# A one-token gated block: ScalarE takes small steps from VectorE, wider value weights, b1 added after the product, a wo tail of twelve rows

## The chip, the cores and the metric

The kernel runs on one core of a Trainium2 chip. The metric is the device time of one execution in microseconds; the median of three runs is 131.92 us (131.88 to 132.19). One core has five engines that run side by side, each with its own program: TensorE (PE; its weight loads are shown apart as PEld), VectorE (DVE), ScalarE (ACT), GpSimd (POOL) and SyncE (SP), which here only issues DMAs. Sixteen DMA engines move data between memory and the core's buffers. Engines wait for each other and for transfers through semaphores.

## What is computed

One token `x` of 576 values goes through two branches that a gate mixes. Branch A is attention over the last 4,096 positions of a key and value cache (32 query heads on 16 key heads, 128 values each). Branch B is a dense layer with GELU, 576 to 4,608 and back. All inputs are bfloat16.

```python
g = sigmoid((x * gate_w).sum(-1))
q = (x @ wq).reshape(heads=32, 128)
k, v = k_cache[:, -4096:], v_cache[:, -4096:]      # 16 heads, each for two query heads
p = softmax(q @ k.T * 128 ** -0.5)
a = (p @ v).reshape(4096) @ wo
h = gelu(x @ w1 + b1)
b = h @ w2 + b2
out = g * a + (1 - g) * b
```

Nearly every byte is read once: 53.6 MB of weights and cache.

## The kernel before

**Stages.** The weights come first: w1 and then wq, each spread over 128 partitions. TensorE multiplies them with `x2`, the token laid out by partition (L404, helper `spread`, four products side by side in column groups of the array). The h row is turned into columns by VectorE (L434), goes through GELU on VectorE and ScalarE (L436 to L460) and ends as `gt`, 36 columns. The q row is turned in the same way and put into `qz_flat`.

**Keys and values.** The 16 key heads are taken in four tiles of four heads (`g` from 0 to 3). For each tile SyncE loads keys (`k_t`) and later values (`v_t`), 4 MB each. VectorE transposes keys in two halves into `kt` (L542), TensorE makes the scores (L564) on top of a product that sets foreign heads to a very low number (L551). `row_max` takes each row's maximum on VectorE (L580), spreads it into 16 columns (`mr`, L583), and TensorE brings it to all rows of a head (L589); `exps` takes the minimum (L597), and ScalarE the exponentials (L601); `probs` transposes them into `pt` (L613). `values(g)` multiplies 32 chunks of weights from `pt`, 32 columns each, with the values (L656), into one bank of 512 columns. `pick(g)` keeps from these only what belongs to each row's own head, with four VectorE operations (L677, L684) and the mask `own4`. `fold(g)` adds up the rows on TensorE (L697) into `o_ps`.

**The end.** The attention result, divided by the sums and times the gate, is made into columns for wo. Of the 128 rows of wo for each head, the first 4 x RW (RW = 30) come as `wo_t`, 30 rows for a partition, and the last RT = 8 rows of each head as `wo_tail`, one partition for each head, in three transfers of 11, 11 and 10 heads (L645). `om` and `om_t` (L766, L771) hold the matching columns; products at L779 and L784 move them into `ov_ps`, and VectorE and ScalarE copy them out as `ov` and `ov_tail`. Then `y_add` (L386) adds vector times matrix row by row into `y_ps`, two products for each of these vectors, one for either half of the 576 outputs. The list `late` sets their order: the vectors of w2's first half that are left (14 to 17), those of `wo_tail`, one product whose result nothing reads (L807), those of `wo_t`, those of w2's second half. ScalarE and VectorE each copy one half of the row out, and SyncE stores it.

**Order.** TensorE and VectorE work off programs whose order is partly set by hand: `queue` chains the emission of each engine's operations in the attention part. Pools with a fixed number of buffers decide when a tile may be loaded: `kt_pool` has two buffers, shared in turn by `rows`, `turn`, the `kt` halves and `wo_tail`; the big tiles go by tags, so that `v_t` of tile 0 takes the place of `k_t` of tile 0, w2 that of `k_t` of tile 2 (before it w1), `v_t` of tile 3 that of `v_t` of tile 0, and `wo_t` that of `v_t` of tile 1. SyncE issues all large transfers in one order: w1, wq, four `k_t`, two `v_t`, half of w2, `v_t` of tile 2, the three of `wo_tail`, `v_t` of tile 3, `wo_t`, and three pieces of w2's second half (vectors 0 to 9, 10 to 15, 16 and 17). ScalarE issues the short rows x, gate_w, b2 and b1.

**b1.** It comes as two rows of 2,304. Eight small products (L404, weights from `ident`) put it into `h_ps` before the products of w1 add to it.

Of the kernel before, what the change touches and what calls it, by code (L numbers as in the profile page):

```python
# [9 lines left out]
FP32 = mybir.dt.float32  # L10
BF16 = mybir.dt.bfloat16
# [7 lines left out]
def kernel(  # L19
# [15 lines left out]
    nc = tc.nc  # L35
# [169 lines left out]

    rows = kt_pool.tile([2, 8192], BF16, name="rows", tag="kt")
    x_row = rows[0:1, 0:D]
    gw_row = rows[0:1, D : 2 * D]
    b2_row = rows[0:1, 2 * D : 3 * D]
    b1_t = rows[0:2, 3 * D : 3 * D + FH]  # L210
    xdup = rows[0:1, 3 * D + FH : 5 * D + FH]
    junk_row = rows[0:1, 5 * D + FH : 6 * D + FH]
    nc.scalar.dma_start(out=x_row, in_=A_x.rearrange("a b d -> (a b) d"))
    nc.scalar.dma_start(out=gw_row, in_=gate_w.rearrange("(o n) -> o n", o=1))
    nc.scalar.dma_start(out=b2_row, in_=B_b2.rearrange("(o n) -> o n", o=1))
    nc.scalar.dma_start(out=b1_t, in_=B_b1.rearrange("(h n) -> h n", h=2))

# [8 lines left out]

    NCC = 2 * NI + 16 + P + 4
    low = const.tile([P, NCC], I32, name="low")
    mask = const.tile([P, NCC], I32, name="mask")
    c0 = 0  # L230
    for base, pattern, keep in (
        (0, [[1, NI], [1, 2]], 1),
        (128, [[-8, 16]], 120),
        (128, [[-1, P]], 7),
        (128, [[-8, 4]], 24),
    ):
        n = 1
        for step, num in pattern:
            n *= num
        nc.gpsimd.iota(low[:, c0 : c0 + n], pattern=pattern, base=base, channel_multiplier=1)  # L240
        nc.gpsimd.memset(mask[:, c0 : c0 + n], keep)
        c0 += n
# [9 lines left out]
    make_identity(nc, ident[:])  # L252
    RW = 30
    RT = P - 4 * RW
    NZ = 512 + 5 * RW + P
    ROWS = NZ + 32 * NI
# [48 lines left out]
    same8 = is0[:, c0 + 16 : c0 + 16 + P]  # L305
    own4 = is0[:, c0 + 16 + P : NCC]
    row_of = zeros[0:HB, ROWS : ROWS + 32 * HB].rearrange("p (r b m) -> p r b m", r=16, b=HB)
# [21 lines left out]

    nc.vector.tensor_copy(  # L330
        out=xdup.rearrange("p (d t) -> p d t", t=2),
# [3 lines left out]
    for i in range(NI):  # L335
# [27 lines left out]
    nc.scalar.activation(out=ge[:], in_=g_ps[:, 0:1], func=ACT.Exp, scale=-1.0)  # L363
    nc.vector.tensor_scalar(out=ge[:], in0=ge[:], scalar1=1.0, scalar2=None, op0=ALU.add)
    g_t = const.tile([P, 1], FP32, name="g_t")
# [5 lines left out]
    b2g = const.tile([1, D], FP32, name="b2g")  # L371
    nc.vector.tensor_scalar(
        out=b2g[:], in0=b2_row, scalar1=omg[0:1, 0:1], scalar2=None, op0=ALU.mult
    )
    gh = const.tile([P, 1, 5], FP32, name="gh")
    nc.vector.tensor_scalar(
        out=gh[:, 0, :], in0=hi5[:], scalar1=g_t[:, 0:1], scalar2=None, op0=ALU.mult
    )

# [23 lines left out]
    def spread(out, lhsT, rhs, start, stop):  # L403
        nc.tensor.matmul(out, lhsT=lhsT, rhs=rhs, start=start, stop=stop, skip_group_check=True)  # L404

    for u in range(2):
        for c in range(4):
            n0 = c * FG + u * FS
            spread(
                h_ps[32 * c : 32 * c + 32, u, 0:FS],  # L410
                ident[0:2, 0:32],
                b1_t[:, n0 : n0 + FS],
                True,
                False,
            )
    QZ = 24
    qz_flat = const.tile([P, QZ + 4 * NG * P + 96], BF16, name="qz_flat")
    nc.gpsimd.memset(qz_flat[:].bitcast(FP32), 0.0)
    for i in range(NI):
        for u in range(2):  # L420
            for c in range(4):
                n0 = c * FG + u * FS
                spread(
                    h_ps[32 * c : 32 * c + 32, u, 0:FS],
                    x2[:, i, :],
                    w1_t[:, i, n0 : n0 + FS],
                    False,
                    i == NI - 1,
                )
    turn = kt_pool.tile([P, 8192], BF16, name="turn", tag="kt")  # L430
    flat = turn[:].bitcast(FP32)
    h_row, h_col, q_col = flat[:, 0:FG], flat[:, FG : FG + 32 * NJ], flat[:, 2048 : 2048 + 512]
    nc.scalar.copy(out=h_row.rearrange("p (u n) -> p u n", u=2), in_=h_ps[:, :, 0:FS])  # L433
    nc.vector.transpose(out=h_col, in_=h_row.rearrange("p (m j) -> p j m", j=NJ))  # L434
    hacc = const.tile([P, NF], FP32, name="hacc")
    nc.vector.tensor_copy(  # L436
        out=hacc[:].rearrange("p (t j) -> p t j", t=2),
        in_=h_col.rearrange("p (j a) -> p a j", a=32)[:, 0:2, :],
    )
    z2 = const.tile([P, NF], FP32, name="z2")  # L440
    nc.vector.tensor_tensor(out=z2[:], in0=hacc[:], in1=hacc[:], op=ALU.mult)
    C0 = 0.7978845608028654
# [12 lines left out]
    nc.scalar.activation(out=e_h[:], in_=u_t[:], func=ACT.Exp, scale=-1.0)  # L455
    nc.vector.tensor_scalar(out=e_h[:], in0=e_h[:], scalar1=1.0, scalar2=None, op0=ALU.add)
    r_t = const.tile([P, NF], FP32, name="r_t")
# [49 lines left out]

    m1 = const.tile([P, 1], FP32, name="m1")
    mr = const.tile([P, 16], FP32, name="mr")
    negm = const.tile([P, 1], FP32, name="negm")  # L510
    sums = const.tile([P, NG, 1], FP32, name="sums")
# [67 lines left out]
    def row_max(g):  # L579
        queue("dve", lambda: nc.vector.reduce_max(out=m1[:], in_=s_ps[g][:], axis=AX.X))  # L580
        queue(
            "dve",
            lambda: nc.vector.tensor_scalar(  # L583
                out=mr[:], in0=hi16[:], scalar1=m1[:, 0:1], scalar2=None, op0=ALU.mult
            ),
        )
        queue(
            "pe",
            lambda: nc.tensor.matmul(  # L589
                mt_ps[:, 16 * g : 16 * g + 16], lhsT=same8, rhs=mr[:], start=True, stop=True  # L590
            ),
        )

    def exps(g):
        queue(
            "dve",
            lambda: nc.vector.tensor_reduce(  # L597
                out=negm[:], in_=mt_ps[:, 16 * g : 16 * g + 16], axis=AX.X, op=ALU.min
            ),
        )  # L600
        nc.scalar.activation(  # L601
            out=p_t[:].rearrange("p c k -> p (c k)"),
            in_=s_ps[g][:],
            func=ACT.Exp,
            bias=negm[:, 0:1],
            scale=SCALE,
            accum_out=sums[:, g, :],
        )
# [34 lines left out]
    for r in range(3):  # L643
        n = min(11, Hq - 11 * r)
        nc.sync.dma_start(  # L645
            out=wo_tail[32 + r : 32 + r + 4 * n - 3 : 4, 0 : RT * D],
            in_=wo_src[11 * r : 11 * r + n, 4 * RW : P, :].rearrange("h j n -> h (j n)"),
        )
    o_ps = ps_m.tile([P, Hq, 1], FP32, name="o_ps", tag="m")

    v_ps, v_own = [None] * NG, {}

    def value_products(g):
        for c in range(32):
            m = c % 4
            last = nc.tensor.matmul(  # L656
                v_ps[g][32 * m : 32 * m + 32, 0:512],
                lhsT=pt[:, g, c, :],
                rhs=v_t[g][:].rearrange("p (x c) d -> p x c d", x=4)[:, :, c, :],
                start=(c < 4),  # L660
                stop=(c >= 28),
                skip_group_check=True,
            )
        return last
# [4 lines left out]

    own_pool = ctx.enter_context(tc.tile_pool(name="own_pool", bufs=2))  # L670

    def pick(g):
        v_own[g] = own_pool.tile([P, Dh], FP32, name="v_own", tag="own")
        parts = v_ps[g][:, 0:512].rearrange("p (x d) -> p x d", x=4)
        queue(
            "dve",
            lambda: nc.vector.tensor_scalar(  # L677
                out=v_own[g][:], in0=parts[:, 0, :], scalar1=own4[:, 0:1], scalar2=None, op0=ALU.mult
            ),
        )  # L680
        for x in range(1, 4):
            queue(
                "dve",
                lambda x=x: nc.vector.scalar_tensor_tensor(  # L684
                    out=v_own[g][:],
                    in0=parts[:, x, :],
                    scalar=own4[:, x : x + 1],
                    in1=v_own[g][:],
                    op0=ALU.mult,
                    op1=ALU.add,  # L690
                ),
            )

    def fold(g):
        queue(
            "pe",
            lambda: nc.tensor.matmul(  # L697
                o_ps[:, 8 * g : 8 * g + 8, 0],
                lhsT=v_own[g][:],
                rhs=same8[:, 0:8],  # L700
                start=True,
                stop=True,
                skip_group_check=True,
            ),
        )
# [5 lines left out]
    probs(NG - 1)  # L711
    pick(0)
    ls = const.tile([P, NG, 8], FP32, name="ls")
# [4 lines left out]
        op=ALU.mult,  # L718
    )
    values(1)  # L720
    fold(0)
# [46 lines left out]
    )  # L768
    for r in range(3):
        n = min(11, Hq - 11 * r)  # L770
        nc.vector.tensor_tensor(  # L771
            out=om_t[:, 32 + r : 32 + r + 4 * n - 3 : 4],
            in0=o_ps[:, 11 * r : 11 * r + n, 0],
            in1=rgh[:, 11 * r : 11 * r + n, 4],
            op=ALU.mult,
        )
    ov_ps = ps_m.tile([P, RO + RT], FP32, name="ov_ps", tag="m")
# [74 lines left out]
```

## Time and profile before

| | |
|---|---|
| median of three runs | 131.92 us (131.88 to 132.19) |
| the profiled execution | 132.06 us, span of its instructions 130.8 us |
| TensorE busy | 72.3 us (55%), 572 products; weight loads 26.2 us, 462 |
| VectorE busy | 59.1 us (45%), 68 instructions |
| ScalarE busy | 9.0 us (7%), 19 instructions |
| GpSimd busy | 10.3 us (8%), 27 instructions |
| read from memory | 53.62 MB, 410 GB/s over the span |
| DMA queue of SyncE | 2,226 packets, 96.1% of the sixteen engines' span |

The span runs from the first to the last instruction of the profiled execution. Busy shares are means over stages with different limits. A line such as `L656` is a line of the kernel before. The clock column gives the share of full speed that TensorE was granted; it is 1.0 or 0.5 here. A landing is the moment at which a transfer's semaphore has its full count; each DMA engine that takes part adds its own count when its packets are written.

### The profile page before, as it was taken

What the parts mean: (1) busy time and instruction counts of PE and PEld (TensorE: products, weight loads), DVE (VectorE), ACT (ScalarE), POOL (GpSimd) and SP (SyncE); (2) the same over time, 40 slices, a digit from 0 to 9 for tenths busy, and PEclk for the clock granted to TensorE, in tenths of its full rate; (3) what the DMA queues carried; (4) which work ended last, traced back from release to release, by engine and by line L of the source; (5) the groups of instructions that cost most, each with busy time, mean ns of one, the idle gap of its engine ahead of it and who ended that gap; (6) DMA issues with size and microseconds to landing.
All of it is one profiled execution on the core that took longest, in us unless ns stands there. A gap on an engine that the chain in (4) does not pass through costs nothing.

```text
span 130.8 us, 1234 instructions
## 1 busy us (share of the span) xinstructions
PE 72.3 (55%) x572; PEld 26.2 (20%) x462; DVE 59.1 (45%) x68; ACT 9.0 (7%) x19; POOL 10.3 (8%) x27
## 2 busy tenths in 40 slices
PE   0002259460003997769949927985100980678794
PEld 0002103130000221211211211132000360234572
DVE  0023300360079979999999995046500050042001
ACT  2100000113000000030011003003000000000001
POOL 5005940000000000000000060000000000000000
PEclk9999999996555799986999995599955586579999
DMA  7999899899999999999989999999999999999970
GB/s 216 495 471 432 375 428 474 361 461 456 401 421 481 411 401 471 421 391 471 441 381 461 461 401 421 423 415 453 461 401 411 471 431 397 476 391 388 416 284 5
DMA packets 2241, 53.70 MB, mean 411 GB/s; under 512 B 278, under 2 KB 282, under 8 KB 540
## 3 DMA queue, kind: packets, MB, share of 16 engines
q1 hardware_dynamic: 2226, 53.61, 96.1%
q8 instruction: 4, 0.07, 0.2%
q10 hardware_dynamic: 10, 0.01, 0.0%
q14 instruction: 1, 0.01, 0.0%
HBM read 53.62 MB, written 0.00 MB: 410 GB/s over the span
## 4 chain that ended last, share of the span: by engine, by line
DMA 61%; DVE 21%; PE 9%; issue 5%; SPq 2%; ACT 1%; DVEq 0%; ACTq 0%
DMA k_t<-in_A_k_cache_dram 34%; DMA w_t<-in_B_w_dram 27%; DVE kt L542 15%; PE s_ps L564 5%; PE v_ps L656 3%; DVE m L580 3%; DVE pt L613 2%; ACT p_t L601 1%; PE y_ps L386 1%; DVE mr L583 1%; SPq L530 0%; SPq L758 0%; SPq L763 0%; ACT out_row L819 0%; DVE negm L597 0%
## 5 line engine op out<-in xcount | busy, mean ns | idle before, releaser
L564 PE MATMUL s_ps<-kt,qz_flat 128*128 128x512 bf16 x128 | 34.9, 433 | 19.4 <-DVE kt L542 12.6
L542 DVE STREAM_TRANSPOSE kt<-k_t 128x4096 f32<-128x4096 f32 x8 | 35.3, 4432 | 8.8 <-DMA k_t<-in_A_k_cache_dram 8.8
L656 PE MATMUL v_ps<-v_t,pt 128*32 128x512 bf16 x128 | 11.0, 505 | 14.8 <-DMA v_t<-in_A_v_cache_dram 13.3
L564 PEld LDWEIGHTS <-qz_flat 128*128 128x128 bf16 x64 | 7.1, 111 | 44.4 <-issue 42.9
L677 DVE TENSOR_SCALAR v_own<-v_ps,is 128x128 f32<-128x128 f32 x4 | 1.4, 338 | 20.0 <-PE v_ps L656 20.0
L601 ACT ACTIVATE p_t<-s_ps,negm 128x1024 bf16<-128x1024 f32 x4 | 4.5, 1114 | 53.8 <-DVE negm L597 53.8
L656 PEld LDWEIGHTS <-pt 128*32 128x32 bf16 x128 | 3.9, 117 | 20.2 <-DMA v_t<-in_A_v_cache_dram 13.4
L336 PE MATMUL xs_ps<-ident,rows 1*128 1x1 bf16 x9 | 0.6, 189 | 12.2 <-POOL ident masks.py:199 12.2
L642 POOL MEMSET wo_tail<- 128x2304 f32 x1 | 2.0, 2017 | 58.2 <-PE s_ps L564 58.2
L580 DVE TENSOR_REDUCE m<-s_ps 128x1 f32<-128x1024 f32 x4 | 4.8, 1196 | 4.0 <-PE s_ps L564 4.0
L386 PE MATMUL y_ps<-w_t,gt 128*1 128x272 bf16 (+1 forms) x72 | 6.0, 288 | 0.2 <-DMA w_t<-in_B_w_dram 0.2
L613 DVE STREAM_TRANSPOSE pt<-p_t 128x1024 bf16<-128x1024 bf16 x4 | 4.9, 1225 | 2.7 <-ACT p_t L601 2.7
L434 DVE STREAM_TRANSPOSE turn<-turn 128x576 f32<-128x576 f32 x1 | 1.3, 1255 | 9.5 <-ACT turn L433 9.5
L820 DVE CAST out_row<-y_ps 1x272 bf16<-1x272 f32 x1 | 0.4, 429 | 10.1 <-PE y_ps L386 10.1
L386 PE MATMUL y_ps<-wo_t,ov 128*1 128x272 bf16 (+1 forms) x60 | 4.0, 286 | 0.8 <-DMA wo_t<-in_A_wo_dram 0.8
L684 DVE SCALAR_TENSOR_TENSOR v_own<-v_ps,is,v_own 128x128 f32<-128x128 f32 x12 | 4.1, 342 | 0.3
L404 PE MATMUL h_ps<-w_t,zeros 128*32 128x288 bf16 x72 | 4.1, 420 | 0.0
L551 PE MATMUL s_ps<-foreign,zeros 4*128 4x512 bf16 x8 | 3.0, 433 | 2.1 <-POOL foreign L319 2.1
L386 PEld LDWEIGHTS <-gt 128*1 128x1 bf16 x72 | 3.7, 85 | 2.1 <-issue 1.1
L404 PEld LDWEIGHTS <-zeros 128*32 128x32 bf16 (+1 forms) x76 | 2.5, 119 | 7.3 <-issue 4.2
L330 DVE COPY rows<-rows 1x1152 bf16<-1x1152 bf16 x1 | 0.7, 748 | 6.9 <-DMA rows<-in_A_x_dram 6.9
L386 PEld LDWEIGHTS <-ov 128*1 128x1 bf16 x60 | 3.4, 84 | 2.0 <-issue 1.6
(78 smaller groups left out, 40.6 us busy)
## 6 DMA issues: line engine op xcount, KB each, us to landing
k_t<-in_A_k_cache_dram SPq DMA_DIRECT2D x4, 4096.0 KB, 37.7
v_t<-in_A_v_cache_dram SPq DMA_DIRECT2D x4, 4096.0 KB, 23.3
w_t<-in_B_w_dram SPq DMA_DIRECT2D x1, 5184.0 KB, 15.0
wq_t<-in_A_wq_dram SPq DMA_DIRECT2D x1, 4608.0 KB, 25.1
wo_t<-in_A_wo_dram SPq DMA_DIRECT2D x1, 4320.0 KB
w_t<-in_B_w_dram SPq DMA_DIRECT2D x1, 2592.0 KB
w_t<-in_B_w_dram SPq DMA_DIRECT2D x1, 1440.0 KB
w_t<-in_B_w_dram SPq DMA_DIRECT2D x1, 864.0 KB
```

The lines of the kernel that those rows point to most:

```text
L386: last = nc.tensor.matmul(y_out[s], lhsT=vec, rhs=row[:, DH:D] if s else row[:, 0:DH], start=start, stop=stop, skip_group_check=True,)
L404: nc.tensor.matmul(out, lhsT=lhsT, rhs=rhs, start=start, stop=stop, skip_group_check=True)
L542: lambda: nc.vector.transpose(out=kt[g, f][:].bitcast(FP32), in_=keys.rearrange("p c d -> p (c d)").bitcast(FP32),),
L551: nc.tensor.matmul(s_ps[g][:, u * 512 : (u + 1) * 512], lhsT=row_of.rearrange("p r b m -> p (r b m)"), rhs=foreign[:].rearrange("p n b -> ...
L564: last = nc.tensor.matmul(s_ps[g][:, u * 512 : (u + 1) * 512].rearrange("p (c k) -> p c k", k=32), lhsT=qz(g, j, 2 * f + half), rhs=kv[:, ...
L580: queue("dve", lambda: nc.vector.reduce_max(out=m1[:], in_=s_ps[g][:], axis=AX.X))
L601: nc.scalar.activation(out=p_t[:].rearrange("p c k -> p (c k)"), in_=s_ps[g][:], func=ACT.Exp, bias=negm[:, 0:1], scale=SCALE, accum_out=s ...
L613: lambda: nc.vector.transpose(out=pt[:, g, :, :].rearrange("p c q -> p (c q)"), in_=p_t[:].rearrange("p c k -> p (c k)"),),
L642: nc.gpsimd.memset(wo_tail[:, 0 : RT * D].bitcast(FP32), 0.0)
L656: last = nc.tensor.matmul(v_ps[g][32 * m : 32 * m + 32, 0:512], lhsT=pt[:, g, c, :], rhs=v_t[g][:].rearrange("p (x c) d -> p x c d", x=4)[ ...
L677: lambda: nc.vector.tensor_scalar(out=v_own[g][:], in0=parts[:, 0, :], scalar1=own4[:, 0:1], scalar2=None, op0=ALU.mult),
L684: lambda x=x: nc.vector.scalar_tensor_tensor(out=v_own[g][:], in0=parts[:, x, :], scalar=own4[:, x : x + 1], in1=v_own[g][:], op0=ALU.mult ...
```

## The change

It has four parts.

1. VectorE's program becomes shorter. Copies, additions of a constant and multiplications by one value for each partition go to ScalarE: `xdup`, `ge`, `b2g`, `gh`, `hacc`, `z2`, `e_h` and `mr`. For this `m1`, `mr` and `negm` get a column of their own for each tile. `pick` is two operations in place of four, and `om_t` is written by two in place of three.
2. For tiles 0 to 2 two chunks of `pt` are one weight of 64 columns. The two chunks' products use the same weight and go into two banks, so the picked result has 1,024 columns with half of them foreign, and `own8` masks eight parts. Tile 3 stays at 32 columns.
3. b1 is loaded as eight rows of 576 to the partitions on which h's parts stand, and VectorE adds it while it copies h out of `h_ps`; the eight products are gone, and so is ScalarE's copy.
4. RW is 29, so RT is 12: `wo_tail` has twelve rows for each head, `wo_t` 29 for each partition. The three `wo_tail` transfers take every third head in place of eleven heads in a row.

```diff
-    b1_t = rows[0:2, 3 * D : 3 * D + FH]
+    b1_t = const.tile([P, FH // 4], BF16, name="b1_t")
+    nc.gpsimd.memset(b1_t[:].bitcast(FP32), 0.0)
...
-    nc.scalar.dma_start(out=b1_t, in_=B_b1.rearrange("(h n) -> h n", h=2))
+    for hh in range(2):
+        nc.scalar.dma_start(
+            out=b1_t[hh : hh + 97 : 32, :],
+            in_=B_b1[hh * FH : hh * FH + FH].rearrange("(c n) -> c n", c=4),
+        )
...
-    RW = 30
+    RW = 29
...
-    nc.vector.tensor_copy(
+    nc.scalar.copy(
         out=xdup.rearrange("p (d t) -> p d t", t=2),
...
-    nc.scalar.copy(out=h_row.rearrange("p (u n) -> p u n", u=2), in_=h_ps[:, :, 0:FS])
+    nc.vector.tensor_tensor(
+        out=h_row.rearrange("p (u n) -> p u n", u=2),
+        in0=h_ps[:, :, 0:FS],
+        in1=b1_t[:].rearrange("p (u n) -> p u n", u=2),
+        op=ALU.add,
+    )
...
-        queue(
-            "dve",
-            lambda: nc.vector.tensor_scalar(
-                out=mr[:], in0=hi16[:], scalar1=m1[:, 0:1], scalar2=None, op0=ALU.mult
-            ),
+        nc.scalar.activation(
+            out=mr[:, g, :], in_=hi16[:], func=ACT.Copy, scale=m1[:, g : g + 1]
         )
...
-            in_=wo_src[11 * r : 11 * r + n, 4 * RW : P, :].rearrange("h j n -> h (j n)"),
+            in_=wo_src[r : r + 3 * n - 2 : 3, 4 * RW : P, :].rearrange("h j n -> h (j n)"),
...
     def value_products(g):
+        keys = v_t[g][:].rearrange("p (x c) d -> p x c d", x=4)
         for c in range(32):
-            m = c % 4
+            if g < NG - 1:
+                m, bank, w = 64 * (c // 2 % 2), c % 2, pt[:, g, c - c % 2 : c - c % 2 + 2, :]
+                size, first = 64, c < 4
+            else:
+                m, bank, w = 32 * (c % 4), 0, pt[:, g, c : c + 1, :]
+                size, first = 32, c < 4
             last = nc.tensor.matmul(
-                v_ps[g][32 * m : 32 * m + 32, 0:512],
-                lhsT=pt[:, g, c, :],
+                v_ps[g][m : m + size, 512 * bank : 512 * bank + 512],
+                lhsT=w.rearrange("p c q -> p (c q)"),
...
     def pick(g):
+        own, n = (own8, 8) if g < NG - 1 else (own4, 4)
+        part, v_own[g] = sets[:, 8 * g : 8 * g + n, :], sets[:, 28 + g, :]
         queue(
             "dve",
-            lambda: nc.vector.tensor_scalar(
-                out=v_own[g][:], in0=parts[:, 0, :], scalar1=own4[:, 0:1], scalar2=None, op0=ALU.mult
+            lambda: nc.vector.tensor_tensor(
+                out=part,
+                in0=v_ps[g][:, 0 : n * Dh].rearrange("p (x d) -> p x d", x=n),
+                in1=own.rearrange("p (x e) -> p x e", e=1).to_broadcast([P, n, Dh]),
+                op=ALU.mult,
             ),
         )
...
+        queue(
+            "dve",
+            lambda: nc.vector.tensor_reduce(
+                out=v_own[g],
+                in_=part.rearrange("p x d -> p d x"),
+                axis=AX.X,
+                op=ALU.add,
+            ),
+        )
```

The picked parts and results live in a new tile `picks`, which takes a buffer of `kt_pool` after the last `kt` half.

## The prediction, made before the changed kernel was run

> **What bounds the kernel now.** I read the page first, then the chain of waits, the timeline from 85 us on, windows cut at the edges of the clock's changes, and the DMA packets and landings.
>
> The slices say that the DMA engines are never idle; the chain ends in a transfer that had waited 35 us in its queue:
>
> ```profile
> DMA  7999899899999999999989999999999999999970
> ...
> DMA 61%; DVE 21%; PE 9%; issue 5%; SPq 2%; ACT 1%; DVEq 0%; ACTq 0%
> ```
> ```profile
> 91.45 0.59 SPq L758
> ...
> 92.08 0.58 SPq L763
> ...
> 92.72 35.20 DMA w_t<-in_B_w_dram
> 127.92 0.04 issue
> 127.96 1.21 PE y_ps L386 x16
> 129.17 0.02 issue
> 129.19 0.40 ACT out_row L819
> ```
>
> So everything in front of 92 us has cover: wo_t is issued at 91.45, but its first packet starts at 109.0. What is made faster on VectorE there moves nothing.
>
> I sorted the packets into sixteen sequences (one per DMA engine: each packet starts as the one before ends, sizes in the order of issue). None pauses by more than 0.03 us from 1 us to its end, and the ends differ. Five engines got no packet of wo_tail (9,216 bytes each), one got two, ten got three: that is how 11, 11 and 10 heads fall. Without an extra, the five end at 125.6 and the ten at about 126.5. Four packets of 16,384 bytes are instruction loads, at 29.88, 83.34, 110.02 and 126.80. The third sits on an engine with three tail rows: load and eight wo_t packets together take it 11.8 us, against 10.25 for the eight elsewhere, so about 1.3 us are lost to the load, and it ends at 128.15. The landing counts agree: the middle one of w2's three late transfers (vectors 10 to 15) has fifteen engines by 127.02 and the last by 127.92. The 127.96 of the chain waits for that single engine. In the same way wo_t has fifteen engines by 121.43, the last at 122.34; v_t of tile 3 has fifteen by 111.22, the last at 112.23, since the load went in just ahead of that engine's final count. The Trainium skill ("Runtime: NRT & Kernel Launch", Instruction fetch mechanics) calls the cost of such a 16 KiB refill mostly hidden; the rows just read differ, and by the page the last landing would be 127.02.
>
> The last stretch is tight on TensorE too:
>
> ```profile
> 112.27 3.60 PE L656 MATMUL v_ps<-v_t,pt 128*32 128x512 bf16 x32 [4.57 <-DMA v_t<-in_A_v_cache_dram]
> ...
> 119.28 1.20 PE L386 MATMUL y_ps<-wo_tail,ov_tail 128*1 128x272 bf16 x16
> ...
> 120.41 1.12 PE L807 MATMUL spare_ps<-p_t,ones 128*128 128x512 f32 x2
> ...
> 122.38 3.65 PE L386 MATMUL y_ps<-wo_t,ov 128*1 128x272 bf16 x57 [0.84 <-DMA wo_t<-in_A_wo_dram]
> ```
>
> From wo_t's landing to 127.71, 80 products take 5.33 us (0.064 each, and 0.2 of drain); only 0.25 us of waiting is left before 127.96.
>
> **The clock there.** Windows of 3.41 us, cut at the edges where the granted clock changed (columns: length, TensorE busy, clock):
>
> ```profile
> 64.68:68.09 3.41, 1.69 (x10) 1.00 1.07 461
> 74.92:78.33 3.41, 1.24 (x8) 1.00 0.92 394
> 78.33:81.74 3.41, 2.49 (x6) 0.50 1.03 442
> 102.22:105.64 3.42, 3.42 (x32) 0.50 1.05 450
> 105.64:109.05 3.41, 1.69 (x19) 1.00 0.96 414
> ```
>
> A window busy for 1.24 us is followed by half clock; so is 105.64's with 1.69 of light products, while 64.68's with 1.69 of wide ones is not. A full window brings the clock back (102.22), 2.49 does not (78.33). So the edge is near half busy. Ahead of wo_t TensorE now idles 0.85 us, and its window holds 2.58: safe.
>
> **The change, part by part.**
>
> *VectorE's shorter program, operations moved to ScalarE.* Gone from VectorE: the copy (0.75), ge (0.15), b2g (0.61), gh (0.46), hacc and z (0.20 each), e_h (0.18), mr (4 x 0.23). ScalarE's price for a 1-partition row of 1,152 isn't shown; by its rows of 1,024 (1.11) and 576 (0.64) it is 0.64 to 1.3, taken as 1.2. The copy then ends near 8.2, and TensorE needs ident at 12.2 first. mr on ScalarE delays the maximum's product, and behind it the next score products, by 0 to 0.3; those wait for the transpose of keys anyway (12.6 us in all). Price 0; without the DMA backlog it would be a few tenths. An 8,192-byte load at 85.37, also an instruction's, costs its engine about 0.7 (it ends at 127.28). If it is VectorE's and goes, that engine ends near 126.5: it is not the last, so 0.
>
> *b1 by VectorE.* Removes 8 products (0.67) and 4 loads. h's products no longer sit behind the foreign products (17.93) and start near 16 instead of 20.08; on ScalarE's queue two DMAs of four 1,152-byte rows replace one of two 4,608-byte rows (0.5 us more to issue, ahead of the table load, which idles till 6.9 anyway). SP's third k_t issue comes earlier, into a full queue: 0. If b1 came late (the four row packets of that queue are 3.1 us apart on one engine), h waits, with k_t not there until 36.7.
>
> *Value products 64 wide, tiles 0 to 2.* 16 loads for 32, but two products at once where four were: 1.91 us at full clock becomes about 3.5 (32 x 0.107), 3.61 at half becomes 6.9. So v0 ends near 89.2, v1 near 94.6 (SP's wo_t issue behind it, 14 us to spare), v2, from 101.24, near 106.9. The pick becomes 1,024 elements out of PSUM and a strided sum: 1.2 each by the maximum's row of the same shape (1.20); the stride has no row, 1.2 to 2.4. With the reciprocal (0.36) fold 2 comes at 109.8 (up to 111.0), still ahead of v_t 3. Price 0; it holds tile 3's products back only past 111.4. Tile 3's own pick is about 1.25 in place of 1.47.
>
> *Twelve tail rows.* On the engines with three rows 3 x 4,608 bytes come on and 8 x 1,152 go: +4,608, at 27 bytes per ns +0.17 us; on the five others -0.34. On the last engine, if it also held b1's row, -0.08. So wo_t's last landing goes to about 122.45 and the deciding w2 landing to about 128.05. After wo_t 94 products are left for 96; before it 24 for 16 (+0.55 us of work).
>
> *What moves the end.* TensorE's program is 61 instructions shorter up to tile 3's products (12 of b1, 48 weight loads, one foreign weight load). It had begun 439 instructions (271 products, 168 loads) when the second load began and 691 at the third, about 252 apart, so I take it that loads follow the instruction count. Before, 691 is the door of tile 3's products. Now the door is 631, so I expect the third load only when those products run, after v_t 3 has landed. That landing then follows the fifteen: 110.9 for plain engines, +0.51 for the larger tail, 111.4 in place of 112.23. Tile 3 starts 0.8 earlier, and its clock is better: v2 now fills 102 to 107 and the y products follow until 109, so 105.64's window is nearly full and the clock stays up to 112.47. It ends near 114.2 (113.4 to 115.05) in place of 115.9. Then 3.3 us to wo_tail as now, less 0.1 (one small product fewer), 1.7 for 24 products, 1.1 for the spare one: done near 120.3 (119.4 to 121.1). wo_t is still held back by the load on its engine, until 122.45. TensorE idles about 2.1 us (1.35 to 3.1) where it idled 0.85. A window across that is busy about 1.3 us, like 74.92's: half clock while the wo products begin.
>
> The price: in 3.41 us at half clock 27 products run in place of 53, 1.65 us lost (0 to 1.7 as the half rate is at best the same, at worst double; value products show 60 against 113 ns, so near the worst). TensorE: 122.5 + 94 x 0.064 + 0.2 = 128.7, + 1.65 = 130.4, against 129.16: +1.2. The profiled execution took 132.06 (span 130.8, 1.3 around it), which gives 133.3; the median of the runs shown is 0.14 lower, so **133.1**. The Trainium skill ("TensorE: Matmul & The Clock Gate", Why this matters for your kernels) warns only of idle gaps over some 3 us; by it 2.1 us is harmless and the sum is the next paragraph's. The windows above decide against it: 74.92's window was idle for 2.2 us. If the window's edges lie elsewhere in other executions, I count offsets: an edge must leave over 1.7 of 2.1 us in one window, 6 offsets in 10; with a gap of 3 nearly all, with 1.35 none.
>
> **Rivals.**
> 1. *Nothing decides but the bytes.* The clock holds (v_t 3 lands as late as now, or the edges are kind). Then TensorE still waits for the one engine: +0.1 to +0.17, **132.0**. For it: the runs before agree within 0.31 us, so edges elsewhere have cost nothing yet. Against: the gap more than doubles.
> 2. *Faster: the load misses the last engine.* If the third load falls on one of the five light engines, wo_t lands near 121.5 and w2 near 127.2. TensorE bounds: 121.6 + 6.0 + 0.2 = 127.8, the last w2 rows land at 127.9 and need 0.3: 128.2, so -1.0, **130.9**. For it: two of four loads did fall there. Against: the number of loads before it is unchanged.
> 3. *Slower by more.* Light products at half clock don't bring it back, as 2.49 didn't at 78.33: all 94 at double cost, 122.5 + 12.2 = 134.7, **137.4**. Against: the stream has no pauses.
>
> **How the numbers follow.** Clock lost once 0.49, rival 1 0.27, rival 2 0.14, rival 3 0.04, other faster (0.3 to 0.5 us through the two products fewer) 0.03, other slower 0.03. A measurement of this kernel tells about 0.3% (0.4 us) from no change. Faster 0.17, same 0.27, slower 0.56. The likeliest case by itself spans 132.5 to 133.8. The range, 131.5 to 133.9, takes in rival 1 and leaves out rivals 2 and 3.
>
> **What would show it.** Right: half clock in the window of wo_t's first products, about 2 us of idle before them, tile 3's products starting near 111.4, the third 16 KB load after 113. Wrong: full clock there, a wait of 0.3 us or more before the last 16 products (rival 1), or the slowest engine ending near 127.3 (rival 2). The forecast fails if tile 3 starts after 112.2 or wo_t lands before 121.8.

## The result: 0.29 us slower, and the profile after

| | before | after |
|---|---|---|
| median of 20 executions each, taken side by side | 131.90 us (131.78 to 132.19) | 132.19 us (131.98 to 132.70) |
| ratio after / before, 95% interval | | 1.002 [1.0013, 1.0027] |
| the profiled execution | 132.06 us, span 130.8 | 132.70 us, span 131.1 |
| a second profiled execution of the same kernel | | 132.08 us, span 130.5 |

The change costs 0.29 us, 0.2%. That is inside the 0.3% called "no change" in the forecast, but the interval lies clear of 1. The forecast was 133.1.

The profiled execution is the longest of the twenty, so the kernel was profiled a second time (experiment 9). Both are read here, because they end differently. First lines of the first profile's page: the granted clock and the DMA share by slices, the DMA queues, and the engines' shares of the chain.

```profile
PEclk9999998657655688888875888888855578678888
DMA  8999899999999999999998999999999998998950
...
q8 instruction: 4, 0.07, 0.2%
q10 hardware_dynamic: 22, 0.01, 0.0%
...
DMA 49%; PE 24%; DVE 22%; issue 2%; ACT 1%; SPq 0%; DVEq 0%; ACTq 0%
```

The DMA engines are as full as before. Three things are new. The chain has 24% of TensorE where before had 9%. From about 20 us on the clock line shows no digit over 8 where the page of before has 9s: the highest clock granted there was 0.85 and not 1.0. And queue q14, which carried one 8,192-byte instruction load in the span of before, is missing from the list. The end of the chain and the timeline of TensorE in the same execution (columns: start, length, what; in brackets the idle time before it and what ended that):

```profile
93.17 29.11 DMA wo_t<-in_A_wo_dram
122.28 0.04 issue
122.32 7.15 PE y_ps L389 x88
129.47 0.02 issue
129.49 0.40 ACT out_row L822
```
```profile
111.53 2.71 PE L657 MATMUL v_ps<-v_t,pt 128*32 128x512 bf16 x32 [0.63 <-DMA v_t<-in_A_v_cache_dram]
...
117.81 1.99 PE L389 MATMUL y_ps<-wo_tail,ov_tail 128*1 128x272 bf16 x24
119.72 1.23 PE L810 MATMUL spare_ps<-p_t,ones 128*128 128x512 f32 x2
...
122.32 4.03 PE L389 MATMUL y_ps<-wo_t,ov 128*1 128x272 bf16 x55 [1.36 <-DMA wo_t<-in_A_wo_dram]
```

From wo_t's landing on, TensorE works without a pause: at 0.85 of the clock its 88 recorded products take 7.15 us, and the middle and the last piece of w2 have landed (127.81, 128.53) when it reaches them. The same two views of the second profile:

```profile
92.48 35.19 DMA w_t<-in_B_w_dram
127.67 0.04 issue
127.71 1.21 PE y_ps L389 x16
128.92 0.02 issue
128.95 0.40 ACT out_row L822
```
```profile
111.39 1.91 PE L657 MATMUL v_ps<-v_t,pt 128*32 128x512 bf16 x32 [0.49 <-DMA v_t<-in_A_v_cache_dram]
...
117.19 2.98 PE L389 MATMUL y_ps<-wo_tail,ov_tail 128*1 128x272 bf16 x24
120.10 1.12 PE L810 MATMUL spare_ps<-p_t,ones 128*128 128x512 f32 x2
...
122.17 3.65 PE L389 MATMUL y_ps<-wo_t,ov 128*1 128x272 bf16 x56 [0.94 <-DMA wo_t<-in_A_wo_dram]
...
127.71 1.20 PE L389 MATMUL y_ps<-w_t,gt 128*1 128x272 bf16 x16 [0.34 <-DMA w_t<-in_B_w_dram]
```

This is the chain of before: it ends in the middle late piece of w2, and the last 16 products wait for it, from 127.71 where before had 127.96. The clock was 1.0 when the wo products began. It had been halved from 116.23 to 119.64, over the tail products (2.98 us). The windows there, cut at the edges where the granted clock changed (columns: window and length, TensorE busy, weight loads, VectorE, ScalarE, GpSimd, then granted clock, DMA share, GB/s):

```profile
109.40:112.82 3.42, 1.82 (x30) 1.05 (x34) 1.28 (x2) 0.00 (x0) 0.00 (x0) 1.00 1.00 429
112.82:116.23 3.41, 1.76 (x31) 1.05 (x16) 2.18 (x5) 0.00 (x0) 0.00 (x0) 1.00 0.94 397
116.23:119.64 3.41, 3.41 (x34) 2.62 (x31) 0.19 (x1) 0.17 (x1) 0.00 (x0) 0.50 1.02 439
119.64:123.05 3.41, 2.46 (x24) 1.36 (x21) 0.00 (x0) 0.00 (x0) 0.00 (x0) 1.00 0.91 385
```

**Where the 0.29 us are.** Each execution has two numbers: its time, and the span from its first to its last instruction. What is left over lies around the span. Medians over all executions:

| | time | span | time less span |
|---|---|---|---|
| before (30 on the chip of experiments 1 to 4) | 131.98 | 130.7 | 1.29 |
| after (20) | 132.19 | 130.6 | 1.58 |
| before (28 on the chip of experiment 9) | 131.93 | 130.6 | 1.29 |
| after (11 on that chip, experiment 9) | 132.12 | 130.5 | 1.60 |

The span has not grown; the rest has, by 0.29 to 0.31. (Spans are on record to 0.1 us; on the chip of experiment 9 the difference in time is 0.19.) In the trace's DMA packets the 8,192-byte load that before has at 85.37 stands at 132.47 in after, 1.4 us behind the end of the span (131.96 in the second profile, whose span ends at 130.5). Experiments 4 to 8 ask whether the 0.29 us belong to that load.

### The profile page after: what moved, and what is told of

Its sections match the earlier page's. It is cut to its first block, busy times and chain, and to the rows that moved or that the text cites. A ratio compares the mean times of both kernels' runs of the same rounds, so it can differ in the third digit from the quotient of the medians.

```text
span 131.1 us, 1181 instructions
## 1 busy us (share of the span) xinstructions
PE 82.2 (63%) x570; PEld 28.2 (22%) x415; DVE 62.3 (48%) x49; ACT 12.6 (10%) x29; POOL 11.5 (9%) x30
## 4 chain that ended last, share of the span: by engine, by line
DMA 49%; PE 24%; DVE 22%; issue 2%; ACT 1%; SPq 0%; DVEq 0%; ACTq 0%
DMA k_t<-in_A_k_cache_dram 27%; DMA wo_t<-in_A_wo_dram 22%; DVE kt L540 18%; PE s_ps L562 12%; PE v_ps L657 6%; PE y_ps L389 5%; DVE m L578 3%; ACT p_t L596 1%; DVE pt L608 1%; DVE negm L592 0%; ACT out_row L822 0%; PE mt_ps L584 0%; SPq L229 0%; DVEq L540 0%; ACTq L596 0%
## 5 line engine op out<-in xcount | busy, mean ns | idle before, releaser
L562 PE MATMUL s_ps<-kt,qz_flat 128*128 128x512 bf16 x128 | 35.8, 442 | 13.7 <-DVE kt L540 9.6
L657 PE MATMUL v_ps<-v_t,pt 128*64 128x512 bf16 (+1 forms) x128 | 17.2, 476 | 9.4 <-DMA v_t<-in_A_v_cache_dram 7.9
L679 DVE TENSOR_TENSOR picks<-v_ps,is 128x1024 f32<-128x1024 f32 (+1 forms) x4 | 4.3, 1086 | 14.5 <-PE v_ps L657 14.5
L657 PEld LDWEIGHTS <-pt 128*64 128x64 bf16 (+1 forms) x80 | 4.3, 121 | 20.0 <-issue 11.0
L637 POOL MEMSET wo_tail<- 128x3456 f32 x1 | 3.0, 2979 | 60.6 <-PE s_ps L562 60.6
L389 PE MATMUL y_ps<-w_t,gt 128*1 128x272 bf16 (+1 forms) x72 | 7.1, 331 | 0.0
L407 PE MATMUL q_ps<-wq_t,zeros 128*32 128x512 bf16 x36 | 4.0, 629 | 4.6 <-DMA wq_t<-in_A_wq_dram 4.6
L688 DVE TENSOR_REDUCE picks<-picks 128x128 f32<-128x1024 f32 (+1 forms) x4 | 6.6, 1650 | 0.1
L407 PEld LDWEIGHTS <-zeros 128*32 128x32 bf16 (+1 forms) x76 | 3.2, 140 | 12.0 <-issue 11.9
L579 ACT ACTIVATE mr<-hi,m 128x16 f32<-128x16 f32 x4 | 1.2, 308 | 34.6 <-DVE m L578 34.6
```

The lines of the kernel that those rows point to most:

```text
L389: last = nc.tensor.matmul(y_out[s], lhsT=vec, rhs=row[:, DH:D] if s else row[:, 0:DH], start=start, stop=stop, skip_group_check=True,)
L562: last = nc.tensor.matmul(s_ps[g][:, u * 512 : (u + 1) * 512].rearrange("p (c k) -> p c k", k=32), lhsT=qz(g, j, 2 * f + half), rhs=kv[:, ...
L579: nc.scalar.activation(out=mr[:, g, :], in_=hi16[:], func=ACT.Copy, scale=m1[:, g : g + 1])
L637: nc.gpsimd.memset(wo_tail[:, 0 : RT * D].bitcast(FP32), 0.0)
L657: last = nc.tensor.matmul(v_ps[g][m : m + size, 512 * bank : 512 * bank + 512], lhsT=w.rearrange("p c q -> p (c q)"), rhs=keys[:, :, c, :] ...
L679: lambda: nc.vector.tensor_tensor(out=part, in0=v_ps[g][:, 0 : n * Dh].rearrange("p (x d) -> p x d", x=n), in1=own.rearrange("p (x e) -> p ...
```

## The experiments

"VectorE +8" means eight instructions more in VectorE's program than after has; before has 19 more. All ratios are to runs of the kernel before on the same chip (its medians there: 131.98, 131.89 and 131.93). Unless something else is said, the edit is made in the kernel after.

| | edit | median us (lowest to highest, count) | ratio [95%] | span | time less span | 8,192-byte load at |
|---|---|---|---|---|---|---|
| 1 | tail of 8 rows | 132.30 (131.62 to 133.69, 11) | 1.004 [1.0013, 1.0066] | 130.7 | 1.62 | 132.02 |
| 2 | before, tail of 12 | 132.68 (132.07 to 132.99, 7) | 1.0051 [1.0032, 1.007] | 131.4 | 1.28 | 86.35 |
| 3 | spare product out | 132.35 (132.04 to 133.34, 12) | 1.0038 [1.0016, 1.0061] | 130.7 | 1.60 | 133.06 |
| 4 | tail in 16 + 16 heads, VectorE -1 | 131.75 (131.62 to 132.55, 12) | 0.9992 [0.9976, 1.0007] | 130.3 | 1.42 | none |
| 5 | 4 with VectorE +1 (length of after) | 131.89 (131.76 to 133.06, 12) | 1.0012 [0.9989, 1.0035] | 130.3 | 1.58 | 132.63 |
| 6 | VectorE -1 | 132.11 (131.81 to 133.13, 12) | 1.0019 [0.9998, 1.0041] | 130.65 | 1.43 | none |
| 7 | VectorE +8 | 131.88 (131.63 to 132.60, 12) | 1.0 [0.9982, 1.0017] | 130.6 | 1.28 | 84.66 |
| 8 | 4 with VectorE +9 | 131.88 (131.38 to 132.66, 12) | 1.0007 [0.9984, 1.003] | 130.55 | 1.28 | 80.77 |
| 9 | none | 132.12 (132.01 to 133.46, 11) | 1.0024 [1.0005, 1.0042] | 130.5 | 1.60 | 131.96 |
| 10 | before, tail in 16 + 16 | 131.77 (131.61 to 131.91, 11) | 0.9985 [0.9976, 0.9994] | 130.5 | 1.31 | 84.74 |
| 11 | all value weights 32 wide | 132.16 (132.05 to 132.63, 11) | 1.002 [1.0011, 1.003] | 130.6 | 1.63 | 131.94 |
| 12 | 8 with three unread products | 131.53 (131.51 to 131.57, 6) | 0.9969 [0.9956, 0.9981] | 130.3 | 1.25 | 80.82 |

### 1. After, with the tail of eight rows

```diff
-    RW = 29
+    RW = 30
-    NZ = 512 + 5 * RW + 1 + P
+    NZ = 512 + 5 * RW + P
```

> The changed kernel with RW back at 30, so eight tail rows for each head; all else as changed. Theory 'bytes on the last engine': 3 x 4,608 bytes less and 8 x 1,152 more on the engine that ends last, 0.17 us less, so 131.9 to 132.0 against 132.19 for the changed kernel; the sixteenth engine's end moves from 128.05 to about 127.9. Rival 'the shorter programs and wide value products cost it': no difference to the changed kernel, 132.2.

Measured 132.30, not the 131.9 to 132.0 of the theory. Taking part 4 back gains nothing. In its profile (132.25 us) TensorE idles 1.51 us before wo_t and the last 16 products start at 127.79, where the second profile of after has 127.71: the tail's bytes are not what the change costs. Seven of the eleven executions lie from 131.62 to 132.35; the other four took 133.28 to 133.69, with spans of 131.7 to 132.0. None of these four was profiled; experiment 3 shows one execution of such a time.

### 2. Before, with the tail of twelve rows

The same two lines the other way round, in the kernel before.

> The kernel before with RW = 29 alone (twelve tail rows, in three runs of heads as before). Theory 'bytes on the last engine': +0.17 us, 132.05 to 132.2 against 131.90; the third 16 KB load stays at about 110 and the last engine ends near 128.3. Rival 'the other three parts cost it': 131.9, no difference.

Measured 132.68, above the 132.05 to 132.2 that was expected, and the slowest median of all. TensorE's timeline:

```profile
112.38 3.38 PE L656 MATMUL v_ps<-v_t,pt 128*32 128x512 bf16 x32 [4.90 <-DMA v_t<-in_A_v_cache_dram]
...
119.34 3.19 PE L386 MATMUL y_ps<-wo_tail,ov_tail 128*1 128x272 bf16 x24
...
122.47 1.12 PE L807 MATMUL spare_ps<-p_t,ones 128*128 128x512 f32 x2
123.52 3.52 PE L386 MATMUL y_ps<-wo_t,ov 128*1 128x272 bf16 x55
```

The third 16,384-byte load is at 109.09 here, ahead of tile 3's values, which therefore start at 112.38. The tail products fall into a half-clock window (118.82 to 122.23) and take 3.19 us, so wo's products start at 123.52 with no wait in brackets: wo_t was there, TensorE was late. Eight products more are harmful where TensorE is already late, and cost nothing in after, where tile 3 starts 0.9 to 1.0 us earlier.

### 3. After, without the product that nobody reads

```diff
-    late.append(None)
```

> The changed kernel without the product that nobody reads ahead of wo's products. TensorE's idle time before them grows from about 1.4 to about 2.6 us. If the edge is near half a busy window, as the forecast took it, the clock is halved there in most executions and the time grows by 1.0 to 1.3 us, to 133.2 to 133.5. Rival 'one such gap doesn't halve the clock' or 'TensorE has slack enough': 132.2, no difference.

This lengthens the idle gap before wo_t. Eight of twelve executions took 132.04 to 132.48 and four 133.28 to 133.34, so the expectation of "most" was too high. The profile caught one of the four: first TensorE's timeline, then windows with the columns given above.

```profile
122.18 5.14 PE L389 MATMUL y_ps<-wo_t,ov 128*1 128x272 bf16 x55 [2.59 <-DMA wo_t<-in_A_wo_dram]
```
```profile
115.26:118.68 3.42, 2.31 (x34) 1.47 (x28) 1.50 (x5) 0.17 (x1) 0.00 (x0) 1.00 0.97 414
118.68:122.09 3.41, 0.91 (x15) 0.48 (x10) 0.00 (x0) 0.00 (x0) 0.00 (x0) 1.00 0.95 403
122.09:125.50 3.41, 3.32 (x29) 2.63 (x30) 0.00 (x0) 0.00 (x0) 0.00 (x0) 0.50 0.95 398
```

That is what the forecast described: a window busy for 0.91 us, then half clock exactly over wo's first products. They take 5.14 us for 55, against 3.65 for 56 at full clock, 1.5 us more; the execution took 133.28, about 1.1 more than the other eight's typical 132.1 to 132.4. So the forecast's mechanism exists and its price is about right, but even with a gap of 2.59 us eight executions of twelve show no such time, which fits window edges that fall elsewhere (these eight were not profiled). Times over 133 become rarer as the gap in the profile shrinks: four in eleven in experiment 1 (1.51 us), two in twelve in experiment 6 (1.27), one in 31 in the kernel after (0.94 to 1.37; 133.46, experiment 9). None of these was profiled. The Trainium skill ("TensorE: Matmul & The Clock Gate", Why this matters for your kernels) warns of idle gaps over some 3 us; here 2.59 us was enough.

### 4. After, with the tail in two transfers of 16 heads

```diff
-    for r in range(3):
-        n = min(11, Hq - 11 * r)
+    for r in range(2):
...
-            out=wo_tail[32 + r : 32 + r + 4 * n - 3 : 4, 0 : RT * D],
-            in_=wo_src[r : r + 3 * n - 2 : 3, 4 * RW : P, :].rearrange("h j n -> h (j n)"),
+            out=wo_tail[32 + r : 32 + r + 61 : 4, 0 : RT * D],
+            in_=wo_src[r : r + 31 : 2, 4 * RW : P, :].rearrange("h j n -> h (j n)"),
```

`om_t` follows in one operation in place of two, which takes one instruction off VectorE.

> The changed kernel with wo's tail in two transfers of 16 heads in place of 11, 11 and 10, so that each of the sixteen engines carries two tail rows. Theory 'bytes on the last engine': the engine with the third 16 KB load carries 13,824 bytes less, 0.51 us; wo lands near 121.8 for 122.3, the deciding w2 piece near 127.3; TensorE and the last w2 piece (128.0 plus 0.3) then bound: 0.5 to 0.8 us less, 131.4 to 131.7. Rival 'the sum of bytes decides, not one engine': 132.2.

Measured 131.75, just above the range expected, with six of twelve at 131.62 to 131.68. Two things moved. With two rows on every DMA engine in place of three, two or none, the last 16 products start at 127.43 and the span is 130.3. And the rest fell from 1.58 to 1.42: this trace has no 8,192-byte load after the kernel's start. The edit had changed VectorE's length by one, which called for the next four.

### 5 to 8. Only VectorE's length

```diff
-    nc.vector.tensor_scalar(
-        out=omg[:], in0=g_t[:], scalar1=-1.0, scalar2=1.0, op0=ALU.mult, op1=ALU.add
-    )
+    for _ in range(9):
+        nc.vector.tensor_scalar(
+            out=omg[:], in0=g_t[:], scalar1=-1.0, scalar2=1.0, op0=ALU.mult, op1=ALU.add
+        )
```

This is experiment 7, on after: `omg` is written nine times, 0.15 us each, before the keys arrive. Experiments 5 and 8 write it twice and ten times in the kernel of experiment 4. Experiment 6 has ScalarE write it (`activation` with scale -1 and bias 1).

> The kernel with the tail in two transfers of 16 (131.75 us, no 8,192-byte load after its span, 1.42 us outside the span), with one VectorE instruction written twice (omg), so VectorE's program has one instruction more, as many as the changed kernel's. Theory 'the length of VectorE's program sets where its last 8,192-byte load falls': the load is back 1.4 us after the span, the time outside the span goes to about 1.6, the total to about 131.95. Rival 'two transfers in place of three, or the even tail, made it go': no load there, 131.7.

> The changed kernel with omg made by ScalarE, so VectorE's program has one instruction less. Theory 'length of VectorE's program': no 8,192-byte load after the span, 1.3 to 1.42 us outside the span for 1.58, the total 131.9 to 132.0 for 132.19. Rival 'bytes on the last engine': 132.2, load still there. The span itself stays at 130.6 by both.

> The changed kernel with omg written nine times, eight instructions more for VectorE, while it has nothing to do (some 1.2 us near 14 us). Theory 'length of VectorE's program': the 8,192-byte load moves from behind the end into the run (before 130 us), 1.3 us outside the span, so the longer program takes 131.85 to 132.0. Rival 'a longer program can't be faster; what counts is the number of instructions': 132.2 or more.

> The kernel with the even tail and VectorE nine instructions longer. Theory: the load falls inside the run, the time outside the span is 1.3 in place of 1.42, the total 131.5 to 131.7, if the load doesn't hit the engine that ends last (then 0.4 more). Rival: no difference to the even tail alone, 131.75.

The rest follows the length of VectorE's program and the load's place, in both families:

| VectorE against after | 8,192-byte load | time less span |
|---|---|---|
| -1 (experiments 4, 6) | none | 1.42, 1.43 |
| 0 (after, 1, 3, 5, 9, 11) | behind the end | 1.58 to 1.63 |
| +8 (7, 8, 12) | at 81 to 85 | 1.25 to 1.28 |
| +18, +19 (10, 2, before) | at 85 to 86 | 1.28 to 1.31 |

From experiment 4 to 5, one instruction more brings the load back, behind the end, and the rest goes from 1.42 to 1.58. From after to 7, eight instructions more move it into the run: q14 is on the page again,

```profile
q14 instruction: 1, 0.01, 0.0%
```

the rest is 1.28, and the kernel with the longer program takes 131.88 for 132.19. So the time around the span is shown to hang on the length of VectorE's program, which sets this load's place. (After and 7 ran on different chips; their ratios to before, 1.002 and 1.0, say the same.)

How the load costs time can be read from the DMA packets. In the six profiles that have it behind the end, its last byte is the last thing on record, and the measured time is 0.29 to 0.30 us less than that end, counted from the first instruction: 133.00 against 132.70 in the first profile of after, 132.38 against 132.08 in the second. Where the load itself is shorter, the time follows: it takes 0.36 us in experiment 5's profile and 0.53 in after's first, and the time less span is 1.44 and 1.62. So the measured time runs on until this load has ended. Why the kernels without the load still have 0.14 more than those with it inside the run stays open.

Of the totals, 5 and 7 came close to what was expected (131.89 for 131.95, 131.88 for 131.85 to 132.0). Experiment 6 took 132.11 for 131.9 to 132.0. Experiment 8 missed: 131.88 for 131.5 to 131.7, because its executions fall into two groups, six from 131.38 to 131.66 and six from 132.10 to 132.66. Experiment 12 asks why.

### 9. After, once more

> The changed kernel as it is, on the chip of the other runs. Theory 'two terms': 1.58 us outside the span with the 8,192-byte load behind it, the span within 0.15 of before's; 132.1 to 132.25. The third 16 KB load after 113, tile 3's products starting at 111.2 to 111.9. The clock ahead of wo's products falls in none or few of the executions (time near 133.2 where it does).

Measured 132.12; the profile is the second one shown above. The granted clock of 0.85 did not come again in this or any of the other profiles.

### 10. Before, with the tail in two transfers of 16 heads

The transfers as in experiment 4, with two operations for `om_t` in place of three.

> The kernel before with its eight-row tail in two transfers of 16 heads. Theory 'bytes on the last engine': the engine with the third 16 KB load carries 9,216 bytes less, 0.35 us; TensorE has 0.25 us of waiting to give up before its last 16 products, so 0.2 to 0.35 us less, 131.55 to 131.7; 1.29 us outside the span. Rival 'one engine's bytes don't decide': 131.9.

Measured 131.77, a gain of 0.15% [0.06, 0.24]: the direction holds, the size is below what was expected. The balance of the tail is worth something by itself with eight rows. With twelve, the median span is 130.3 in experiments 4 and 5 and 130.5 to 130.6 in after.

### 11. After, with all value weights 32 wide

```diff
-            if g < NG - 1:
+            if False:
-        own, n = (own8, 8) if g < NG - 1 else (own4, 4)
+        own, n = own4, 4
```

> The changed kernel with 32-column value weights and 512-element picks in all tiles (part two undone), the same number of VectorE instructions. Theory 'the third load follows TensorE's instruction count': with 48 weight loads more ahead of tile 3 it falls near 110 again, tile 3's products start near 112.4 to 112.8, and with 24 tail products TensorE is late for wo as in the kernel before with twelve rows: 132.6 to 133.0. Rival 'wide products don't matter': 132.2, tile 3 at 111.5.

The expectation missed. The time is that of after (132.16), the third load stays at 115.14, and tile 3 starts no later:

```profile
111.43 3.61 PE L657 MATMUL v_ps<-v_t,pt 128*32 128x512 bf16 x32 [3.71 <-DMA v_t<-in_A_v_cache_dram]
...
122.18 3.65 PE L389 MATMUL y_ps<-wo_t,ov 128*1 128x272 bf16 x56 [0.79 <-DMA wo_t<-in_A_wo_dram]
```

Part 2 of the change costs no time and brings none: tile 3's products run at half clock here (3.61 us, 1.91 in the second profile of after), and wo's products start as there, at 122.18. The 48 weight loads are not needed to move the third load either: without part 2, TensorE's program up to tile 3 is only 13 instructions shorter than before's, and the load still comes behind the start of tile 3's products. It comes when TensorE has begun 752 instructions (427 products, 325 weight loads); in after it was 717, in before 691. So a fixed count, as the prediction took it, doesn't place this load. What does stays open.

### 12. The even tail, a longer VectorE program, three unread products

To experiment 8 come three products of 512 columns between the last rows of w2's first half and tile 3's fold, where TensorE otherwise waits for `pick`; nobody reads them.

```diff
+    spare_ps = ps_s.tile([P, 1024], FP32, name="spare_ps", tag="s")
+    for n in range(3):
+        queue(
+            "pe",
+            lambda: nc.tensor.matmul(
+                spare_ps[:, 512:1024],
+                lhsT=ident[:],
+                rhs=v_t[3][:, 0:4, :].rearrange("p c d -> p (c d)"),
+                start=True,
+                stop=True,
+            ),
+        )
```

> The kernel with the even tail and the longer VectorE program (e8), with three products of 512 columns that nobody reads between tile 3's last w2 products and its fold, where TensorE waits for the pick. Theory 'the executions near 132.5 lost the clock in a window that was little over half busy': they vanish or become rare, median 131.45 to 131.65, below both kernels. Rival 'those come from something else, or the products delay the fold': median 131.9 or more.

Experiments 4, 5 and 8 had executions 0.5 to 1.3 us above their lowest ones. One was caught in the profile of experiment 5 (132.70). Its windows, then those of experiment 12:

```profile
115.70:119.11 3.41, 1.97 (x29) 1.16 (x23) 2.21 (x5) 0.17 (x1) 0.00 (x0) 1.00 1.09 465
119.11:122.53 3.42, 3.42 (x27) 2.28 (x26) 0.00 (x0) 0.00 (x0) 0.00 (x0) 0.50 0.86 363
```
```profile
115.92:119.33 3.41, 2.86 (x36) 1.58 (x30) 1.50 (x4) 0.17 (x1) 0.00 (x0) 1.00 0.96 411
119.33:122.74 3.41, 2.89 (x33) 1.70 (x29) 0.00 (x0) 0.00 (x0) 0.00 (x0) 1.00 0.93 394
```

In experiment 5 a window with 1.97 us of mostly light products was not enough: half clock followed (in before a window with 2.00 us, from 115.88, kept the clock), and wo's products began at 123.39, late and without waiting. In 12 the same stretch holds 2.86, and the clock stays. Its end, in the timeline:

```profile
121.82 3.65 PE L390 MATMUL y_ps<-wo_t,ov 128*1 128x272 bf16 x56 [0.52 <-DMA wo_t<-in_A_wo_dram]
...
127.39 1.20 PE L390 MATMUL y_ps<-w_t,gt 128*1 128x272 bf16 x16 [0.36 <-DMA w_t<-in_B_w_dram]
```

All six executions lie within 0.06 us of one another, at 131.53: faster than before by 0.31% [0.19, 0.44] and than after by some 0.6 us. Six executions are few, but their highest, 131.57, is below the lowest of after's 31 (131.98) and of before's 28 beside it (131.76).

## Why the prediction was wrong

**"TensorE idles about 2.1 us ... half clock while the wo products begin ... +1.2".** This is the step that failed. It put 1.2 us into a sum that came out 0.9 too high; the other 0.3 is the load below, which the sum left out. In the second profile of after the gap is 0.95 us, the wo products begin at clock 1.0 and take 3.65 us for 56, and the last 16 products start at 127.71, where before had 127.96: the term of +1.2 measured nothing. The gap of the first profile is 1.37 us. By the prediction's own count of window edges a gap of 1.35 loses the clock at no edge.

What led up to the gap was forecast well. The third 16,384-byte load did move, from 110.02 to 115.28 (115.13 in the second profile), behind the start of tile 3's products, though not at the count of instructions given (experiment 11). In the first profile these started at 111.53 (forecast 111.4, before 112.27), ended at 114.24 (forecast 114.2), and wo_t landed at 122.28 (forecast 122.45). That the end agrees is partly luck: this profile ran at 0.85 of the clock; in the second they ended at 113.30.

The gap came out shorter than forecast because TensorE had more to do in front of it. In the first profile the spare product ended at 120.95 and not at 120.3. `pick` and its sum on tile 3 take 0.69 + 1.02 where 1.25 was put, so the tail's products started 0.4 us later than forecast after tile 3; and the 24 tail products took 1.99 at the clock of 0.85, for 1.7. In the second profile the half-clock window came earlier, over those same tail products (2.98 us), where wo_t's own lateness still covers it: a lost clock ahead of the gap shortens the gap. The forecast let the clock fall in one place only.

The price of a lost clock was sized rightly (1.65 put, 1.5 measured in experiment 3), and so was the threshold near half a window: 2.31 and 2.46 us kept the clock, 1.97, 1.92 and 0.91 lost it. Near the threshold it is not sharp; in the second profile a window with 1.82 kept it and the next one, with 1.76, lost it. The row that the prediction set against a limit of 3 us does not carry its point: the 2.2 us of idle time in 74.92's window are part of a gap of 3.10 us. Two others do: the window of the same trace from 54.44 to 57.85 is busy for 1.44 us, its longest gap is 1.97 us, and half clock follows; and experiment 3, where the gap is 2.59.

**The load priced at nothing.** The forecast saw that the 8,192-byte load at 85.37 might be VectorE's and might go, asked only what its DMA engine would gain, and put 0. The load did not go. It moved behind the end of the program, where nothing covers it: 1.29 became 1.58 around the span. With the span unchanged, this is what was measured (experiments 5 to 8).

**A slip in the working.** The load of 16,384 bytes and eight wo_t packets take 11.81 us on their engine and eight packets 10.25 elsewhere. That is 1.56 us lost, where the prediction says about 1.3. Its sum goes by the landings and doesn't use the figure.

**The value products at price 0**: right (experiment 11). The strided sum (one that adds values lying 128 apart) was put at 1.2 to 2.4 for 1,024 elements and cost 1.86. VectorE's groups in the first profile of after, with the sums on top of the row maximum of the same shape (columns: count, busy us, mean ns, idle before):

```profile
L688 DVE TENSOR_REDUCE picks<-picks 128x128 f32<-128x1024 f32 x3 | 5.6, 1859 | 0.1
...
L578 DVE TENSOR_REDUCE m<-s_ps 128x1 f32<-128x1024 f32 x4 | 4.8, 1204 | 1.7 <-PE s_ps L562 1.6
...
L688 DVE TENSOR_REDUCE picks<-picks 128x128 f32<-128x512 f32 x1 | 1.0, 1023 | 0.0
```

Fold 2 ran at 110.50, still ahead of v_t 3 and inside the forecast's 109.8 to 111.0. The 1.02 for 512 elements is the one that mattered.

**b1 at price 0**: held in the trace, though no run undoes it alone. h's products start at 16.61 (forecast near 16, before 20.08), and q's behind them wait for wq, till 26.10.

**The tail's bytes, +0.17 on the last engine**: not seen. The last 16 products start at 127.71 in the second profile of after and 127.79 with eight rows (experiment 1), in before at 127.96. What the rows cost on one engine was not separated further.

**Rival 1, "nothing decides but the bytes", 132.0**: the nearest time, for another reason. The end of the span was as it said, set by w2's middle piece with no loss of clock, but the bytes added nothing and the 0.29 us came from outside the span. **Rival 2** (the load misses the last engine) did not happen: the span is not shorter by its 1.0 us. Experiments 4, 10 and 12 reach part of that gain with balanced engines instead. **Rival 3** did not happen: the halved clock came back after one window, in experiment 3 too.

## What to carry to other kernels

Compare the time less the span before looking for a difference inside the span: a program that is made shorter can push an engine's last instruction load behind the end, where it costs more than the removed instructions brought. When several DMA engines share the end, deal short rows out evenly before asking how many bytes they are. And a forecast of the clock has to ask where each half-clock window will fall: ahead of a late transfer it was free here, behind it it cost 1.5 us of TensorE's time and about 1.1 of the total.

## What the runs showed of the hardware

- An 8,192-byte instruction load 1.4 us behind the last instruction goes with 0.29 to 0.35 us more time (1.58 to 1.63 around the span, against 1.28 with the load inside the run), and the measured time follows the load's end in all six profiles that have it there. The Trainium skill ("Runtime: NRT & Kernel Launch", Instruction fetch mechanics) calls the cost of crossing a boundary of 16 KiB mostly hidden; the load of 8 KiB in these runs is not hidden where it falls behind the end.
- A sum over the outer of two axes, with 128 values between neighbours, takes 1.86 us for 1,024 elements a partition and 1.02 for 512, where a maximum over 1,024 neighbours takes 1.20.
- One of the fourteen profiled executions was granted at most 0.85 of the clock in place of 1.0; TensorE then set the end (7.15 us without a pause behind wo_t), and it was the longest of its twenty. Nothing in the runs tells why.
